# A frequency-domain mixer and a hash-routed expert layer on one core: mixed rows in token order, gathered by lists of token numbers

## The chip, the cores and the metric

The kernel runs on one core of one Trainium2 chip. The metric is the device time of one execution in microseconds, the median of three timed runs. The profile is of one further execution, whose span (first to last instruction) is somewhat shorter than the timed figure.

## The reference

Eight batches of 2496 tokens with 256 channels are filtered along the sequence: a real FFT, a product with a complex filter per frequency and channel, and the inverse FFT. The 19968 mixed rows then go through one of eight experts, chosen by the token's number alone.

```python
X = np.fft.rfft(x, axis=1)                     # x: (8, 2496, 256)
Y = X * (filt_r + 1j * filt_i)[None]
rows = np.fft.irfft(Y, n=2496, axis=1).reshape(19968, 256)

expert_idx = token_ids * 2654435761 % 8        # the low three bits of token_ids, in another order
for e in range(8):
    mask = expert_idx == e
    out[mask] = np.maximum(rows[mask] @ w1[e], 0.0) @ w2[e]      # 256 -> 1024 -> 256, float32
```

## The kernel before

**Mixing.** 2496 is 39 times 64, so each transform is done as matmuls with small tables, in four products per batch: `pa` (stage 1), `pb` and `pc` (stage 2, with the filter between them) and `pd` (stage 3). Between them the data goes through DRAM (`d1`, `d2`), because the next product needs another axis in the partitions: `load1` brings x, `load2` brings `d1`, `load4` brings `d2`. One batch has 44 matmuls of 256 columns in `pa`, 40 in `pb`, 40 in `pc` and 44 in `pd`.

**Routing.** From the token numbers the vector engine counts tokens per expert and gives each token a slot, so that the tokens of one expert lie in tiles of 128 rows. There are 163 tiles. Rows without a token (896 of them) are filled by seven scatters of a blank. The tiles are put in four groups (in the code: stages, by `STAGES = (2, 4, 6, 8)`): a tile of the first group holds tokens of the first two batches alone, one of the second group tokens of the first four, and so on, so that the expert layer can begin when two batches are mixed.

**Stage 3 and the scatter.** Each result row is written with a tag (its own token number, 16 words wide) straight to its slot in `xs`, a row of 272 words. GpSimd issues one indirect DMA for 117 rows:

```python
def stage3(self, u):
    n = min(XG, HN + 1 - XG * u)
    o = opool.tile([NR, XG, W], F32, ...)              # W = 256 + 16, two buffers
    nc.vector.tensor_scalar(o[:, 0:n, C:].bitcast(I32), tokno[...], float(self.b * S), None, op0=OP.add)
    copy = nc.scalar.copy if self.b < 2 else nc.vector.tensor_copy
    self.products(wi_t, ..., o, copy, u, "pd")
    for i in range(n):                                 # four per unit, 22 per batch
        scatter(o[0:r, i, :], sidx[0:r, self.b, j:j + 1], f"xs_{self.b}")
```

**The tiles.** A tile is loaded with one plain DMA, transposed (`xps`, `xt`), multiplied up (`ups`: 32 matmuls of 128 columns), put through the ReLU (`ht`), multiplied down (`dps`: 16 matmuls of 256 columns) and scattered to the output by the tags that came with it. Pieces of the mixing of the later batches lie between the two products:

```python
def load(i):
    q = tiles[i]
    xg[i] = gath.tile([P, W], F32, ...)                # eight buffers
    ld = nc.sync.dma_start(out=xg[i][:], in_=xs[q * TB:(q + 1) * TB, :])
    # waits for the batches of the tile's group, not for later ones

for i in range(NT):
    if i + 4 < NT:
        load(i + 4)
    up(i, ht)
    weights(i + 2, 0)                                  # loaded only where the expert changes
    if i + 1 < NT:
        turn(i + 1)
    while main and main[0][0] < i + 1:                 # pieces of mixing, by a table of times
        main.pop(0)[1]()
    down(i, ht)                                        # ends with the scatter to out, on GpSimd
    weights(i + 2, 1)
```

**Before the first tile** lies everything with a negative time in a table, in order: the mixing of batches 0 and 1, stage 1 of batch 2 and the first three units of its stage 2, the routing, and the load of the first two experts' weights.

```python
for v in range(NV):
    batches[0].load1(v)                                # x of batch 0 on the sync queue
...
todo = part1(0, spaced(-153, -143, NU)) + [(-152.5, count), (-152.4, route)]
todo += [(-154, lambda: load_tables(0)), (-129.5, places)]      # tables and filters on GpSimd and ACT queues
todo += part2(0, spaced(-128, -95, N_2), -142)
todo += part1(1, spaced(-123.5, -105, NU), [-141.5, -135, -134.5])   # last list: when x of batch 1 is loaded
todo += [(-118.2 + .1 * i, lambda i=i: (weights(i, 0), weights(i, 1))) for i in range(2)]
todo += part2(1, spaced(-94, -60, N_2), -103) + part3(0, spaced(-84, -51, NU), -94.5)
todo += part3(1, spaced(-54, -21, NU), -62) + part1(2, spaced(-52, -19, NU), [-85, -80, -41])
...
todo += part2(2, [-16, -12, -8] + spaced(.1, 5.5, N_2 - 3), -18) + part2(3, spaced(8.5, 15.5, N_2), 7)
```

Of the kernel before, what the change touches and what calls it, by code (L numbers as in the profile page):

```python
# [11 lines left out]
F32 = mybir.dt.float32  # L12
# [29 lines left out]

TB = 128
NT = (N + E * (TB - 1)) // TB
W = C + 16
NJ = N // P
# [50 lines left out]
def route_table():  # L97


    t = np.zeros((P, G + 2 + NQP + HN + 1), np.float32)  # L100
    p = np.arange(P)
    r = np.arange(NR)
    t[:NR, G + 2 + NQP:] = (N2 * (r % N1) + np.array(H0)[r // N1])[:, None] + np.arange(HN + 1)
    for g, b in enumerate(STAGES):
        t[:, g] = p < b * S // NJ
    order = sum(stage_tiles(), []) + [NT] * (2 * P - NT)
    t[:, G:G + 2] = np.array(order).reshape(2, P).T
    t[:, G + 2:G + 2 + NQP] = p[:, None] * NQP + np.arange(NQP)
    return t
# [3 lines left out]
def kernel(  # L113
# [16 lines left out]

    xs = nc.dram_tensor("xs", (NT * TB, W), F32)
    slot_dram = nc.dram_tensor("slots", (N,), I32)
# [22 lines left out]
    sidx = keep.tile([NR, B, HN + 1], I32)  # L155
    tokno = keep.tile([NR, HN + 1], F32)
# [7 lines left out]
    class Batch:  # L164


        def __init__(self, b):
            self.b = b
            self.d1 = self.d2 = None
            self.x, self.t2, self.t4, self.p = {}, {}, {}, {}  # L170
            self.g = None
# [112 lines left out]
        def stage3(self, u):  # L284

            n = min(XG, HN + 1 - XG * u)
            o = opool.tile([NR, XG, W], F32, name=f"o_{self.b}_{u}", tag="o")
            nc.vector.tensor_scalar(o[:, 0:n, C:].bitcast(I32),
                                    tokno[:, XG * u:XG * u + n].unsqueeze(2).to_broadcast([NR, n, W - C]),
                                    float(self.b * S), None, op0=OP.add)  # L290
# [4 lines left out]
            for i in range(n):  # L295
                j = XG * u + i
                r = NR if j < HN else N1
                scatter(o[0:r, i, :], sidx[0:r, self.b, j:j + 1], f"xs_{self.b}")

    def scatter(rows, index, group):  # L300
        st = nc.gpsimd.indirect_dma_start(  # L301
            out=xs[:], out_offset=bass.IndirectOffsetOnAxis(ap=index, axis=0),
            in_=rows, in_offset=None, bounds_check=NT * TB - 1, oob_is_err=False)
        for other in ["xs_pad", "xs_read"] + [f"xs_{b}" for b in range(B)]:
            tc.declare_no_dep(st.ins, group=other, reason="distinct rows")
        tc.add_to_no_dep_group(group, st.ins)

# [28 lines left out]
    tok = rpool.tile([P, NJ, 2], I32)  # L336
    nc.scalar.dma_start(tok[:], tok_h.bitcast(I32).rearrange("(p j two) -> p j two", p=P, two=2))
    rt = rpool.tile([P, G + 2 + NQP + HN + 1], F32)
    nc.scalar.dma_start(out=rt[:], in_=r_dram.ap())
    nc.vector.tensor_copy(tokno[:], rt[0:NR, G + 2 + NQP:])  # L340
# [3 lines left out]
    def load_tables(part):  # L344
        sl = S_PARTS[part]
        nc.gpsimd.dma_start(out=d_t[:, sl, :], in_=d_dram.ap()[:, sl, :])
        for k in range(2):
            load_filter(k, sl)

    def load_filter(k, sl):  # L350
        filt = (filt_r, filt_i)[k]
        for q in range(2):
            off, step = (0, C) if q == 0 else (N1 * C, -C)
            (nc.gpsimd if k or sl.start else nc.scalar).dma_start(
# [17 lines left out]
    make_identity(nc, ident[:])  # L372
    sign = rpool.tile([P, 1], F32)
# [17 lines left out]
    def count():  # L391

        eid_i = rpool.tile([P, NJ], I32)
        nc.vector.tensor_scalar(eid_i[:], tok[:, :, 0], E - 1, None, op0=OP.bitwise_and)
        eid = rpool.tile([P, NJ], F32)
        nc.vector.tensor_copy(eid[:], eid_i[:])
        mask = rpool.tile([P, E, NJ], F32)
        nc.vector.tensor_tensor(mask[:], eid[:].unsqueeze(1).to_broadcast([P, E, NJ]),
                                over(iota_e[:], NJ), op=OP.is_equal)
        maskf = mask[:].rearrange("p e j -> p (e j)")  # L400
        run = rpool.tile([P, E, NJ], F32)
        nc.vector.tensor_tensor_scan(run[:].rearrange("p e j -> p (e j)"),
                                     ones[:, 0:1].to_broadcast([P, E * NJ]), maskf, 0.0,
                                     op0=OP.mult, op1=OP.add)
        ends = rpool.tile([P, E + 1], F32)
        nc.vector.memset(ends[:, 0:1], 0.0)
        nc.vector.tensor_copy(ends[:, 1:], run[:, :, NJ - 1])
        cnt = rpool.tile([P, E], F32)
        nc.vector.tensor_sub(cnt[:], ends[:, 1:], ends[:, 0:E])
        cntg = rpool.tile([P, G, E], F32)  # L410
        nc.vector.tensor_tensor(cntg[:], cnt[:].unsqueeze(1).to_broadcast([P, G, E]),
                                rt[:, 0:G].unsqueeze(2).to_broadcast([P, G, E]), op=OP.mult)
        ps = fps.tile([P, 2, C], F32, name="cnt_ps", tag="f")
        nc.tensor.matmul(out=ps[:, 0, 0:G * E], lhsT=ones[:, 0:P], rhs=cntg[:].rearrange("p g e -> p (g e)"),
                         start=True, stop=True)
        nc.tensor.matmul(out=ps[:, 1, 0:E], lhsT=before[:], rhs=cnt[:], start=True, stop=True)

        rv.update(eid=eid, eid_i=eid_i, mask=mask, run=run, ends=ends, ps=ps)

    def route():  # L420
# [4 lines left out]
        nc.vector.tensor_copy(upto[:].rearrange("p g e -> p (g e)"), ps[:, 0, 0:G * E])  # L425
# [25 lines left out]
        base = rpool.tile([P, E], F32)  # L451
        nc.vector.tensor_sub(base[:], ps[:, 1, 0:E], ends[:, 0:E])
# [4 lines left out]
        acc = rpool.tile([P, E, NJ], F32)  # L457
        tmp = mask
        for e in range(E):
            nc.vector.scalar_tensor_tensor(run[:, e, :], run[:, e, :], base[:, e:e + 1], mask[:, e, :],  # L460
# [236 lines left out]
```

## Time and profile before

| what | value |
|---|---|
| timed, median of three (lowest, highest) | 1643.16 us (1642.09, 1643.37) |
| span of the profiled execution | 1629.8 us |
| TensorE matmul busy | 1518.8 us, 93% of the span |
| VectorE, ScalarE, GpSimd busy | 539.0, 217.1, 355.7 us |
| first matmul | at 15.7 us |
| first tile's first `ups` matmul | at 207.7 us |
| indirect DMAs by GpSimd | 176 to `xs`, 7 blanks, 163 to `out` |

"Busy" counts the time in which an engine executes; an engine that waits is not busy. A row of the profile's groups names a source line, the engine, the operation, what it writes and reads, how often it ran, its total and mean time, and then the idle time of the engine just before it with what ended that. The clock is TensorE's granted clock, 1.00 being full speed. A DMA share of 1.00 means that all 16 DMA engines are occupied.

### The profile page before, as it was taken

Reading aid. Unit: us, or ns where it says so; the run is one execution under the profiler, and the core shown is the slowest. Engines: PE = TensorE matmul, PEld = TensorE weight load, DVE = VectorE, ACT = ScalarE, POOL = GpSimd, SP = SyncE. Lnnn points to the kernel's source line nnn. Section 1 sums busy time; section 2 is a strip of 40 time slices with the busy share of each in tenths; the row PEclk is TensorE's granted clock in tenths of the full one; section 3 lists DMA queues with packets and bytes.
Section 4 is the critical chain, followed back from the end, with each engine's and each line's share of the span. In section 5 each row is a group of like instructions: output and inputs, shape, how many; then the busy total and the mean of one; then the engine's idle time right before and its main releaser. Section 6 shows DMA issues by size and latency. Waiting matters only on the chain.

```text
span 1629.8 us, 26685 instructions
## 1 busy us (share of the span) xinstructions
PE 1518.8 (93%) x9522; PEld 1381.7 (85%) x9522; DVE 539.0 (33%) x1022; ACT 217.1 (13%) x371; POOL 355.7 (22%) x375
## 2 busy tenths in 40 slices
PE   3676589999999999999999999999999999999997
PEld 2554378988888999899989998999999999999997
DVE  6572142452244444233434442222122121221221
ACT  2322212112111111111111111000000000000000
POOL 0235300331320132122121322233111111111111
PEclk9788699999999999999999999999999999999999
DMA  7998627747864883674537643544152413132220
GB/s 189 306 290 244 198 98 205 240 165 207 245 218 150 244 256 111 194 197 147 185 114 222 199 135 115 147 127 162 45 203 79 140 37 126 52 94 88 84 84 9
DMA packets 152541, 258.77 MB, mean 159 GB/s; under 512 B 16185, under 2 KB 118508, under 8 KB 150410
## 3 DMA queue, kind: packets, MB, share of 16 engines
q1 hardware_dynamic: 103345, 163.46, 33.1%
q0 software_dynamic: 21136, 50.96, 9.4%
q10 hardware_dynamic: 27928, 42.65, 8.3%
q8 instruction: 76, 1.25, 0.3%
q14 instruction: 56, 0.45, 0.1%
HBM read 431.87 MB, written 86.09 MB: 318 GB/s over the span
## 4 chain that ended last, share of the span: by engine, by line
PE 42%; issue 36%; POOL 7%; DMA 3%; DVE 2%; POOLq 1%; ACT 0%; SPq 0%; ACTq 0%; DVEq 0%
PE ups L630 15%; PE dps L642 15%; POOL out_dram L646 6%; PE pb L240 3%; PE pa L203 3%; PE pc L263 3%; PE pd L203 2%; POOL xs L301 2%; DMA xs<-o,sidx 1%; PE xps L619 1%; DVE z L250 1%; PE pa L198 0%; POOLq L646 0%; DMA d<-g 0%; DVE y L247 0%
## 5 line engine op out<-in xcount | busy, mean ns | idle before, releaser
L630 PEld LDWEIGHTS ups<-xt,w 128*128 128x128 f32 x5216 | 610.3, 193 | 9.2 <-DVE xt L621 1.0
L630 PE MATMUL ups<-xt,w 128*128 128x128 f32 x5216 | 611.1, 276 | 0.6 <-DVE xt L621 0.6
L642 PE MATMUL dps<-w,ht 128*128 128x256 f32 x2608 | 591.0, 380 | 0.0
L642 PEld LDWEIGHTS dps<-w,ht 128*128 128x128 f32 x2608 | 490.0, 191 | 63.7 <-issue 1.6
L646 POOL DMA_INDIRECT out_dram<-osb,xg x163 | 159.6, 979 | 944.6 <-DVE osb L645 919.4
L636 DVE TENSOR_SCALAR ht<-ups 128x512 f32<-128x512 f32 x163 | 112.8, 692 | 526.8 <-PE ups L630 519.7
L634 ACT ACTIVATE ht<-ups 128x512 f32<-128x512 f32 x163 | 97.3, 597 | 1008.0 <-PE ups L630 992.3
L301 POOL DMA_INDIRECT xs<-o,sidx x176 | 175.3, 996 | 245.7 <-DVE o L205 145.7
L645 DVE COPY osb<-dps 128x256 f32<-128x256 f32 x163 | 69.3, 425 | 404.5 <-PE dps L642 396.2
L240 PE MATMUL pb<-t,d_t 128*128 128x256 f32 x320 | 91.1, 413 | 23.8 <-DMA t<-d 23.3
L250 DVE TENSOR_TENSOR z<-pb,filt 64x512 f32<-64x512 f32 x160 | 110.1, 688 | 2.2
L263 PE MATMUL pc<-y,e_t 128*128 128x256 f32 x320 | 90.1, 407 | 19.7 <-DVE y L251 19.3
L240 PEld LDWEIGHTS pb<-t,d_t 128*128 128x128 f32 x320 | 63.5, 209 | 35.5 <-issue 25.9
L263 PEld LDWEIGHTS pc<-y,e_t 128*128 128x128 f32 x320 | 63.3, 203 | 35.8 <-issue 17.5
L203 PE MATMUL pd<-t,wi_t 120*117 120x256 f32 x320 | 81.2, 399 | 11.7 <-DMA t<-d 7.1
L203 PEld LDWEIGHTS pd<-t,wi_t 120*117 120x117 f32 x320 | 58.9, 191 | 25.5 <-issue 9.1
L247 DVE TENSOR_TENSOR y<-pb,filt 128x512 f32<-128x512 f32 x80 | 55.3, 691 | 68.3 <-PE pb L240 67.8
L266 ACT COPY g<-pc 128x512 f32<-128x512 f32 x80 | 46.8, 585 | 233.2 <-PE pc L263 229.8
L621 DVE COPY xt<-xps 128x256 f32<-128x256 f32 x163 | 67.6, 415 | 1.9 <-PE xps L619 1.9
L619 PE MATMUL xps<-ident,xg 128*128 128x128 f32 x326 | 62.6, 274 | 3.1 <-DMA xg<-xs 3.1
L203 PE MATMUL pa<-x,wf_t 117*120 117x256 f32 x264 | 63.3, 383 | 0.6 <-DVE z L250 0.6
L205 ACT COPY t<-pa 120x512 f32<-120x512 f32 x80 | 46.0, 588 | 90.6 <-PE pa L203 88.1
(102 smaller groups left out, 352.5 us busy)
## 6 DMA issues: line engine op xcount, KB each, us to landing
w<-in_moe_w_dram SPq DMA_DIRECT2D x322, 1024.0 KB
xg<-xs SPq DMA_DIRECT2D x163, 136.0 KB
t<-d SPq DMA_DIRECT2D x80, 256.0 KB
d<-g ACTq DMA_DIRECT2D x80, 256.0 KB
d<-t ACTq DMA_DIRECT2D x16, 960.0 KB
t<-d SPq DMA_DIRECT2D x16, 960.0 KB
x<-in_x_dram SPq DMA_DIRECT2D x39, 312.0 KB
x<-in_x_dram SPq DMA_DIRECT2D x21, 234.0 KB
```

The lines of the kernel that those rows point to most:

```text
L203: nc.tensor.matmul(out=ps[0:cols * H, k, :], lhsT=w[:], rhs=src[:, 2 * i + k, :], start=True, stop=True)
L240: nc.tensor.matmul(out=ps[:, i, :], lhsT=d_t[:, s, :], rhs=self.t2[s // SG][:, s % SG, :], start=True, stop=True)
L250: nc.vector.tensor_tensor(out=z[b], in0=ps[a], in1=f_t[1][a, sl, :], op=OP.mult)
L263: nc.tensor.matmul(out=ps[:, i, :], lhsT=e_t[:, 2 * u + i, :], rhs=pr[:, i, :], start=True, stop=True)
L301: st = nc.gpsimd.indirect_dma_start(out=xs[:], out_offset=bass.IndirectOffsetOnAxis(ap=index, axis=0), in_=rows, in_offset=None, bounds_ch ...
L619: nc.tensor.transpose(out=ps[:, dp, :], in_=xg[i][:, dp * P:(dp + 1) * P], identity=ident[:])
L630: nc.tensor.matmul(out=ps[:, k, :], lhsT=w1[:, dp, fp * P:(fp + 1) * P], rhs=xt[i][:, dp, :], start=(dp == 0), stop=(dp == DP - 1))
L634: nc.scalar.activation(out=dst, in_=ps[:], func=AF.Relu)
L636: nc.vector.tensor_scalar_max(dst, ps[:], 0.0)
L642: nc.tensor.matmul(out=ps[:], lhsT=ht[:, fp, :], rhs=w2[:, fp, :], start=(fp == 0), stop=(fp == FP - 1))
L645: nc.vector.tensor_copy(out=o[:], in_=ps[:])
L646: st = nc.gpsimd.indirect_dma_start(out=out[:], out_offset=bass.IndirectOffsetOnAxis(ap=xg[i][:, C:C + 1].bitcast(I32), axis=0), in_=o[:], ...
```

## The change

The mixed rows are stored in token order with plain DMAs from the scalar engine's queue, three for a unit of four rows. What is scattered instead is a list: one entry of 16 words for each slot, which holds the token's number. A tile loads its list (two tiles' lists in one plain DMA) and gathers its 128 rows with an indirect DMA; the same list then serves the scatter to the output. The lists depend on the token numbers alone, so they can be written before any row is mixed. For this the routing counts by pairs of batches (`G` = 4 groups of 39 columns instead of 156 columns in one), and the lists of one pair are 39 indirect DMAs of 128 entries. The schedule ahead of the first tile is laid out anew: the second part of the tables waits for x, x of batch 1 is asked for early, the weights later, and no stage 2 of batch 2 comes before the first tile.

```diff
-W = C + 16
-NJ = N // P
+LW = 16
+NJ = N // (4 * P)
...
-    xs = nc.dram_tensor("xs", (NT * TB, W), F32)
-    slot_dram = nc.dram_tensor("slots", (N,), I32)
+    mixed = nc.dram_tensor("mixed", (N + 1, C), F32)
+    lists = nc.dram_tensor("lists", (NT * TB, LW), I32)
... stage 3
-            o = opool.tile([NR, XG, W], F32, name=f"o_{self.b}_{u}", tag="o")
-            nc.vector.tensor_scalar(o[:, 0:n, C:].bitcast(I32), ...)
+            o = opool.tile([NR, XG, C], F32, name=f"o_{self.b}_{u}", tag="o")
-            for i in range(n):
-                scatter(o[0:r, i, :], sidx[0:r, self.b, j:j + 1], f"xs_{self.b}")
+            last, self.o = self.o, (o, u)
+            if last and self.b >= 2:
+                self.store3(*last)
+            if self.b < 2 or u == NU - 1:
+                self.store3(o, u)
+        def store3(self, o, u):
+            for h in range(H):
+                st = nc.scalar.dma_start(out=... mixed, rows of 4 KB ..., in_=o[N1 * h:N1 * h + N1, 0:n, :])
+    def listed(g, j0, j1):
+        if j0 == 0:
+            nc.gpsimd.iota(number[:], pattern=[[1, NJ], [0, LW]], base=P * NJ * g, channel_multiplier=NJ)
+        for j in range(j0, j1):
+            scatter(number[:, j, :], slots[:, g, j:j + 1], f"lists_{g}")
... tables
+        eng = nc.sync if part == 0 else nc.gpsimd
+        if part:
+            nc.gpsimd.tensor_copy(junk[:], batches[0].x[1][0:1, 0, 0:1])     # waits for x
... the table of times
-    todo = part1(0, spaced(-153, -143, NU)) + [(-152.5, count), (-152.4, route)]
-    todo += [(-154, lambda: load_tables(0)), (-129.5, places)]
+    todo = part1(0, spaced(-155, -143, NU)) + [(-152.5, count), (-152.4, route), (-152.3, places)]
+    todo += [(-154.9, lambda: load_tables(0)), (-154.8, lambda: load_tables(1))]
-    todo += part1(1, spaced(-123.5, -105, NU), [-141.5, -135, -134.5])
-    todo += [(-125, tile_experts), (-121, experts), (-108, blanks)]
+    todo += part1(1, spaced(-129, -105, NU), [-150, -149, -136])
+    todo += [(-140, tile_experts), (-130, experts), (-60, blanks)]
+    todo += [(-142, lambda: listed(0, 0, NJ))]
-    todo += [(-118.2 + .1 * i, lambda i=i: (weights(i, 0), weights(i, 1))) for i in range(2)]
-    todo += part2(1, spaced(-94, -60, N_2), -103) + part3(0, spaced(-84, -51, NU), -94.5)
-    todo += part3(1, spaced(-54, -21, NU), -62) + part1(2, spaced(-52, -19, NU), [-85, -80, -41])
+    todo += [(-82 + .1 * i, lambda i=i: (weights(i, 0), weights(i, 1))) for i in range(2)]
+    todo += part2(1, spaced(-100, -70, N_2), -103) + part3(0, spaced(-92, -73, NU), -97)
+    todo += part1(2, spaced(-70, -60, NU), [-104, -103.9, -78]) + part3(1, spaced(-59.5, -48, NU), -66)
-    todo += part2(2, [-16, -12, -8] + spaced(.1, 5.5, N_2 - 3), -18) + ...
+    todo += part2(2, spaced(.1, 7.4, N_2), -40) + ...
-    todo += part3(2, spaced(7, 14, NU), 5.6) + ...
+    todo += part3(2, spaced(8, 14, NU), 7.5) + ...
+    for g, (t0, t1) in enumerate([(1, 23), (30, 62), (70, 102)]):
+        todo += [(t, lambda g=g, j=j: listed(g + 1, j, j + 1)) for j, t in enumerate(spaced(t0, t1, NJ))]
... the tiles
-        xg[i] = gath.tile([P, W], F32, name=f"xg_{i}", tag="xg")
-        ld = nc.sync.dma_start(out=xg[i][:], in_=xs[q * TB:(q + 1) * TB, :])
+        if i % 2 == 0:
+            lst[i] = gath.tile([P, 2, LW], I32, name=f"lst_{i}", tag="lst")
+            ld = nc.sync.dma_start(out=lst[i][:, 0:n, :], in_=... lists of tiles i and i + 1 ...)
+        xg[i] = gath.tile([P, C], F32, name=f"xg_{i}", tag="xg")           # six buffers
+        ld = nc.gpsimd.indirect_dma_start(
+            out=xg[i][:], out_offset=None, in_=mixed[0:rows, :],
+            in_offset=bass.IndirectOffsetOnAxis(ap=lst[i // 2 * 2][:, i % 2, 0:1], axis=0), ...)
```

## The prediction

> **What bounds the kernel now.** I read the table of stretches first, then the groups of instructions, then the chain of waits and the timeline around the first tile.
>
> The table of stretches gives, for each stretch, its length, busy time and count of each engine, the granted clock, the DMA share and the rate. I set the borders at the places where the work changes:
>
> ```profile
> 0.00:40.00 40.00, 15.81 (x56) 12.20 (x56) 24.73 (x70) 10.84 (x16) 3.29 (x14) 0.94 0.71 187
> 40.00:125.00 85.00, 62.21 (x224) 47.37 (x224) 56.22 (x96) 23.80 (x38) 24.94 (x30) 0.83 0.95 300
> 125.00:150.00 25.00, 14.49 (x46) 9.86 (x46) 8.27 (x15) 5.41 (x11) 14.64 (x15) 0.75 0.81 244
> 150.00:182.00 32.00, 21.01 (x82) 15.78 (x81) 1.32 (x6) 11.17 (x22) 20.61 (x21) 0.87 0.71 208
> 182.00:207.70 25.70, 10.85 (x27) 6.49 (x26) 8.71 (x13) 1.99 (x5) 1.09 (x2) 0.57 0.65 204
> ...
> 222.00:700.00 478.00, 465.35 (x2888) 422.45 (x2887) 186.56 (x332) 74.69 (x130) 111.24 (x112) 1.00 0.64 198
> 700.00:1157.00 457.00, 452.38 (x2945) 418.32 (x2944) 153.94 (x290) 49.24 (x84) 116.71 (x118) 1.00 0.50 154
> 1157.00:1617.00 460.00, 460.00 (x3184) 434.44 (x3183) 91.64 (x190) 38.21 (x64) 62.22 (x64) 1.00 0.28 90
> ```
>
> There are two regimes. From 222 us on TensorE is busy nearly without a break (its first number against the length: 465 of 478, 452 of 457, 460 of 460), the DMA share is at most 0.64, and nothing but TensorE work counts. Before 207.7 us TensorE is busy for 124 us, at a lowered clock, and the DMA engines are full for the middle 85 us (0.95).
>
> The groups tell what a tile is made of, and how GpSimd stands:
>
> ```profile
> L630 PE MATMUL ups<-xt,w 128*128 128x128 f32 x5216 | 611.1, 276 | 0.6 <-DVE xt L621 0.6
> L642 PE MATMUL dps<-w,ht 128*128 128x256 f32 x2608 | 591.0, 380 | 0.0
> L646 POOL DMA_INDIRECT out_dram<-osb,xg x163 | 159.6, 979 | 944.6 <-DVE osb L645 919.4
> L301 POOL DMA_INDIRECT xs<-o,sidx x176 | 175.3, 996 | 245.7 <-DVE o L205 145.7
> L619 PE MATMUL xps<-ident,xg 128*128 128x128 f32 x326 | 62.6, 274 | 3.1 <-DMA xg<-xs 3.1
> ```
>
> TensorE waited 3.1 us in all for a tile's rows, so loads are hidden in the main part. In the timeline the first `ups` matmuls of successive tiles without mixing are 7.245 us apart, and eight mixing matmuls add 1.72 to 1.73 us, or 0.2155 us each. Over the main part this adds up: 163 tiles at 7.245 us are 1181 us; of the 6 x 168 = 1008 mixing matmuls of batches 2 to 7, 44 + 20 were done before, so 944 at 0.2155 us are 203 us; together 1384 us. The measured stretch from 207.7 to the end of the last `dps` near 1620.5 is 1413 us. So 29 us are other losses, of which 3.9 are in the first tile, at a cold clock, and most of the rest in tiles that hold two units of stage 2 one after the other. There is little to gain in the main part; **the change has to pay ahead of the first tile**.
>
> There the chain of waits names the scatters:
>
> ```profile
> 147.42 7.23 DMA xs<-o,sidx
> ...
> 162.35 7.05 DMA xs<-o,sidx
> ...
> 174.58 5.51 DMA xs<-o,sidx
> ...
> 185.16 4.27 DMA d<-t
> ...
> 190.54 3.18 DMA t<-d
> ...
> 201.63 4.66 DMA xg<-xs
> ```
>
> In this view each line is start, length, what. Stage 3 of batch 1 (147 to 182 us) writes into two buffers `o`, and a buffer is free only when its four scatters have been issued (one every 1.3 us: 0.99 busy and 0.30 until the next) and have landed. From 185 us on the chain is the write and reload of `d1` of batch 2 for three units of stage 2, then the tile's own load, which stands on the sync queue behind them.
>
> **What the Trainium skill says.** "DMA: Bandwidth & Descriptors", section "Issuing engines are not separate DMA queues", says that transfers issued by different engines all run on the same 16 DMA engines and interleave; moving the row stores from GpSimd to the scalar engine's queue thus saves issue time, not transfer time. The trace agrees for 40 to 125 us, where three queues together stand at a share of 0.95. The same page's "Specifications" puts transfers under 512 B below line rate, because the engine then reads, modifies and writes. A list entry is 64 B; no run here shows its cost yet. "TensorE: Matmul & The Clock Gate", section "What's actually happening", says that the clock halves after an idle window of about 3.4 us; the trace agrees, with 0.57 granted from 182 to 207.7 us, where waits of 9.5 and 3.1 us lie between TensorE's pieces.
>
> **The change part by part.**
>
> *First matmul.* It waits for x until 15.7 us while about 1.5 MB of tables and filters are asked for by other queues at the same time. At the 187 GB/s of that stretch, x of the first third (0.94 MB) plus a fair part of the rest is what takes so long. With the tables behind x I expect the first matmul near 10 us: -5.
>
> *Stage 2 of batch 0.* Before, its matmuls run from 41 us to 107 in the timeline, with the second half of the filters arriving at 63 to 68 us and x of batch 1 asked for at 38 to 51. Both now come earlier, and 4 MB of weights come later. I take its end at 92 us: -15, the -5 above included.
>
> *Stage 3 of batch 1.* Before, six units in 35 us. After, a unit has copies of 1.1 us, three store issues of about 0.5 us, and a landing of about 4 us (the write of `d1` took 4.27), and two buffers: (1.1 + 1.5 + 4) / 2 = 3.3 us a unit, 20 us in all: -15, of which I count 14.
>
> *From the last row to the first tile.* Before, 25.7 us (182 to 207.7). After, the last store lands (4 us), the gather is issued (1.3), lands (3.7, the median landing of the scatters to `xs`), and transpose and copy take 1.2 as now: about 11 us, -14.
>
> *Given back.* Three units of stage 2 of batch 2 (20 matmuls) move behind the first tile: +4.3 in the main part. Lists: 39 scatters at 1.3 us are 51 us on GpSimd; GpSimd is idle for most of 40 us to 110 us, so this lies beside other work, but they are 4992 small writes in the stretch where DMA is full. Weights (4.2 MB, 14 us at 300 GB/s) now fall into stage 2 of batch 1. I give back 16 us for both.
>
> Sum ahead of the first tile: -15 - 14 - 14 + 16 = -27, so it starts at 181 us. As a check by bytes: the stretches sum to 51.0 MB up to 207.7 us. The new order needs about 49.5 (blanks -1.0, tags -0.3, x of batch 3 less, lists +0.35). By 181 us that is a mean of 273 GB/s, below the 300 of the full stretch and above the 246 of before. At 300 GB/s it would be 165 us, at 246 it would be 201.
>
> *Main part.* GpSimd gets two indirect DMAs a tile instead of one, and while lists are written (39 in 22 tiles) 1.8 more: 3.8 x 1.3 = 4.9 us of at least 7.245. A gather is asked for four tiles ahead, some 29 us, and needs 2 + 1.3 + 4. The vector engine loses 48 tag writes (9.2 us), off the path. The scalar engine gains 18 issues a batch, and is at 13%. I take 0 for all this.
>
> Time: 1643.2 - 27 + 4.3 = 1620.5, rounded to **1621 us**.
>
> **Rivals.** (1) *DMA takes the place of the scatters.* If the transfers ahead of the first tile run at the old mean, because the lists' small writes cost as much as whole rows, the tile starts near 200 us and the time is 1640. For it: share 0.95 for 85 us. Against it: the share falls to 0.71 and 0.65 after 150 us, where the new order has no scatter to wait for. (2) *GpSimd becomes the bound.* Its queue is in order, and a gather stands behind list scatters and behind the scatter to the output of an earlier tile, which waits for that tile's end. If a gather came late by 1 us in each tile, it would cost 163 us. The lead of four tiles speaks against it; a loss at the three borders between groups, of up to 10 us each, is likelier (1650). (3) *The full rate is kept.* With no landing to wait for, the stretch runs at 300 GB/s, the tile starts at 165 us and the time is 1605.
>
> **Range and chances.** The start lies between 164 and 202 us by these, which is 1603 to 1642. Faster by over 2% needs less than 1610.3, a start before 170.5: 0.22. Slower by over 2% (above 1676) needs rival 2 in full: 0.04. Within 2%: 0.74.
>
> **What would show it.** The first `ups` matmul near 181 us; a first `pa` near 10 us; no wait of a copy for a scatter in stage 3, but short ones for stores to `mixed`; a DMA share of 0.85 or more up to 150 us; tiles still 7.245 us apart, with under 5 us in all of TensorE waiting for `xg`. The prediction is wrong if the share is near 1 and the start is still about 200, if tiles after 222 us are longer than 7.245, or if TensorE waits at tiles 30, 70 or 108.

## The result: slower by 4.3%, and the profile after

The changed kernel takes **1712.53 us** (median of four runs, 1707.16 to 1716.71) against 1642.62 us before (four runs, 1639.85 to 1643.37): 1.0427 times as long, 95% interval 1.0394 to 1.0460. The prediction was 1621 us, with a range up to 1642. It was wrong in sign: the change made the kernel slower.

The table of stretches of the kernel after, in the columns known from before (start and end, length, busy time of TensorE, its weight loads, VectorE, ScalarE and GpSimd, granted clock, DMA share, GB/s):

```profile
0.00:40.00 40.00, 14.58 (x56) 10.89 (x56) 29.66 (x73) 9.58 (x16) 7.72 (x20) 0.81 0.85 238
...
60.00:80.00 20.00, 0.21 (x1) 0.00 (x0) 1.40 (x3) 0.58 (x1) 15.38 (x16) 0.56 0.04 9
...
92.00:136.00 44.00, 29.06 (x106) 21.48 (x105) 23.84 (x33) 15.21 (x23) 1.73 (x3) 0.77 0.78 261
136.00:191.00 55.00, 39.80 (x125) 28.83 (x126) 29.34 (x50) 11.62 (x22) 0.00 (x0) 0.78 0.59 163
191.00:247.70 56.70, 27.86 (x91) 19.25 (x89) 0.42 (x1) 13.13 (x25) 10.32 (x11) 0.71 0.73 211
...
700.00:1200.00 500.00, 492.22 (x3165) 452.07 (x3164) 168.38 (x298) 57.92 (x100) 173.66 (x171) 1.00 0.51 153
```

The stretch from 60 to 80 us has no counterpart before: TensorE works for 0.21 us of 20, the DMA engines are at a share of 0.04, and GpSimd alone is busy, issuing list scatters (15.38 us). The stretch from 136 to 191 is stage 2 of batch 1. In the kernel before, the same work lies here:

```profile
98.00:135.00 37.00, 28.48 (x114) 22.18 (x112) 28.25 (x44) 10.25 (x18) 15.14 (x15) 0.93 0.89 278
```

VectorE does about the same in both (29.34 and 28.25 us), but in 55 us instead of 37, and with the DMA engines at 0.59 instead of 0.89: the stage now waits for something other than transfers at full rate. TensorE, with a granted clock of 0.78 instead of 0.93, is busy for 39.80 us instead of 28.48.

The groups of instructions of the kernel after:

```profile
L658 PE MATMUL ups<-xt,w 128*128 128x128 f32 x5216 | 611.6, 276 | 0.7 <-DVE xt L649 0.7
L670 PE MATMUL dps<-w,ht 128*128 128x256 f32 x2608 | 596.6, 382 | 5.8 <-DMA w<-in_moe_w_dram 4.7 <-issue 1.1
L636 POOL DMA_INDIRECT xg<-mixed,lst x163 | 173.3, 1063 | 387.7 <-DMA lst<-lists 140.1 <-issue 77.1 <-PE pa L198 38.9
L304 POOL DMA_INDIRECT lists<-number,slots x156 | 155.6, 997 | 72.2 <-issue 47.0 <-DVE slots L495 24.3 <-POOL number L314 0.8
L647 PE MATMUL xps<-ident,xg 128*128 128x128 f32 x326 | 62.5, 274 | 7.1 <-DMA xg<-mixed,lst 7.1
```

The tiles cost what they cost before. The gathers wait 140.1 us for their lists on GpSimd, but TensorE waits only 7.1 us in all for gathered rows (3.1 before). New is the wait of `dps` for weights (4.7 us; it was 0.0 for anything).

The chain of waits ahead of the first tile (start, length, what) names where the time lies:

```profile
13.99 20.28 DMA d<-t
...
67.96 21.85 another core or an unknown queue
...
146.19 8.13 DMA d<-g
...
177.50 2.83 DMA mixed<-o
180.36 14.71 issue
...
199.09 13.49 DMA t<-d
...
219.51 6.21 DMA t<-d
225.74 5.11 DMA mixed<-o
...
232.82 4.78 DMA mixed<-o
...
243.43 2.78 DMA xg<-mixed,lst
```

The write of `d1` of batch 0 takes 20.28 us. The 21.85 us at 68 are in the stretch where everything stands still. At 146 a store to `mixed` waits for an earlier store to `d2`. From 180 on, SyncE's queue stands at the last third of x of batch 2, with the read of `d2` of batch 1 behind it; the loads of x are issued from 195.07 on, the read at 199.09, and it takes 13.49 us to land. Not all of the 14.71 us are lost to the order: the last stores to `d2` are issued at 191.47, and by the semaphore records they had landed near 194.5, so the read was held some 4.6 us by x. The last step, from gather to tile, is short.

By the first and last matmul of each product, and with the start of the first tile's `ups`, the same in a table (the last column is a further run of the changed kernel, e9, told below):

| step | before | after | e9 |
|---|---|---|---|
| first `pa` | 15.7 | 8.0 | 10 |
| end of stage 2 of batch 0 | 98 | 130 | 96 |
| end of stage 2 of batch 1 | 135 | 191 | 168 |
| start of stage 3 of batch 1 | 148 | 212.7 | 190.9 |
| last matmul of stage 3 of batch 1 starts | 181.1 | 238.6 | 216.5 |
| first `ups` | 207.7 | 247.7 | 225.7 |

The first tile is 40 us later than before. The timed medians differ by 70 us, which leaves 30 for what follows. But the old kernel's profiled execution took 1631.37 us, 11 less than its median, so profile against profile what follows is 45 us longer; where those 11 us lie is not recorded.

### The profile page after: what moved, and what is told of

Its sections match the earlier page's. It is cut to its first block, busy times and chain, and to the rows that moved or that the text cites. A ratio compares the mean times of both kernels' runs of the same rounds, so it can differ in the third digit from the quotient of the medians.

```text
span 1715.1 us, 27107 instructions
## 1 busy us (share of the span) xinstructions
PE 1538.2 (90%) x9522; PEld 1388.9 (81%) x9522; DVE 534.9 (31%) x970; ACT 216.8 (13%) x371; POOL 508.9 (30%) x515
## 4 chain that ended last, share of the span: by engine, by line
PE 82%; DMA 7%; issue 4%; DVE 3%; another core or an unknown queue 2%; ACT 1%; SPq 1%; ACTq 0%; POOL 0%; POOLq 0%; DVEq 0%
PE ups L658 33%; PE dps L670 32%; PE pd L198 4%; PE pc L258 4%; PE pa L198 4%; PE pb L235 3%; DMA d<-t 2%; DMA t<-d 2%; PE xps L647 2%; DVE z L245 1%; DMA mixed<-o 1%; DMA d<-g 1%; DVE y L242 1%; PE pd L193 0%
## 5 line engine op out<-in xcount | busy, mean ns | idle before, releaser
L674 POOL DMA_INDIRECT out_dram<-osb,lst x163 | 161.8, 993 | 628.3 <-DVE osb L673 603.7
L636 POOL DMA_INDIRECT xg<-mixed,lst x163 | 173.3, 1063 | 387.7 <-DMA lst<-lists 140.1
L304 POOL DMA_INDIRECT lists<-number,slots x156 | 155.6, 997 | 72.2 <-issue 47.0
L198 PE MATMUL pd<-t,wi_t 120*117 120x256 f32 x320 | 87.9, 422 | 17.2 <-DMA t<-d 7.6
```

The costliest lines, as they stand in the source:

```text
L198: nc.tensor.matmul(out=ps[0:cols * H, k, :], lhsT=w[:], rhs=src[:, 2 * i + k, :], start=True, stop=True)
L304: st = nc.gpsimd.indirect_dma_start(out=lists[:], out_offset=bass.IndirectOffsetOnAxis(ap=index, axis=0), in_=rows, in_offset=None, bounds ...
L636: ld = nc.gpsimd.indirect_dma_start(out=xg[i][:], out_offset=None, in_=mixed[0:rows, :], in_offset=bass.IndirectOffsetOnAxis(ap=lst[i // 2 ...
L674: st = nc.gpsimd.indirect_dma_start(out=out[:], out_offset=bass.IndirectOffsetOnAxis(ap=lst[i // 2 * 2][:, i % 2, 0:1], axis=0), in_=o[:], ...
```

## The experiments

Each group of runs below shared one chip and one run of the kernel before on it; the groups ran on different chips, so kernels are compared within a group only. All but g1 are single runs, and differences under some 5 us are not read.

### Group 1: are the list scatters, and their small rows, what costs? (before: 1633.36)

**e1 and e2**: the kernel before with 39 more scatters (of 64-byte rows in e1, of 1088-byte rows in e2) to a spare tensor, between `places` and the weights on GpSimd's queue.

```diff
-(-129.5, places)
+(-129.5, places), (-129.4, burst)      # 39 indirect DMAs of 128 rows, 16 or 272 words each
```

> The kernel before, with 39 indirect scatters of 128 rows of 64 bytes added right after the slots are known, into a DRAM tensor that nothing reads (nothing is left out). Theory L (a run of small list writes holds up the other engines): a gap of 20 to 35 us in which DVE, ACT and TensorE stand still while GpSimd scatters, signals of TensorE that reach their waiters about 10 us late, first tile 20 to 35 us later than 207.7 us, time about 1665 to 1680. Theory T (order of tables and x alone is to blame for the later start): no gap, time within 10 us of before, since GpSimd's 50 us lie beside other work. In both the weights of the first experts come about 50 us later than before, which should not reach the first tile.

> The same 39 scatters, with rows of 1088 bytes instead of 64 (the size of the rows that the kernel before scatters to xs). If the smallness of the rows is what holds the engines up (theory L): no gap with late signals, but 5.4 MB more traffic in the full stretch, some 18 us at 300 GB/s, time about 1655 to 1662. If it is the run of 39 scatters without a pause, whatever their size: the same gap as with 64 bytes or a longer one, time 1670 or more.

Measured: 1658.54 and 1659.89 us, first `ups` at 235.2 and 236.6. A run of 39 scatters costs 25 us, and the size of the rows costs nothing that can be seen. "DMA: Bandwidth & Descriptors", section "Specifications", of the Trainium skill puts transfers under 512 B below line rate; at one scatter in 1.28 us these runs show no difference between 64 B and 1088 B. What costs is what stands behind: in e1 the weights are issued at 114 us instead of 57, land beside stage 2 and 3, and the next row scatters, which signal the same semaphores, wait for them (14.4 us in three waits). Those row scatters free the buffers of stage 3, and TensorE waits 27.3 us at one `pb` for the copies into them. The changed kernel has no row scatters, so this cost is not its own.

**e3**: the changed kernel without list and blank scatters; five plain DMAs at the start fill the lists in slot order, so the tiles gather the rows of other tokens, and rows go to wrong experts. The amount of work in the tiles is unchanged.

```diff
-            scatter(number[:, j, :], slots[:, g, j:j + 1], f"lists_{g}")
+    nc.gpsimd.dma_start(out=lists[...], in_=number[:, 0:n, :])      # five of these, no scatter
```

> The kernel after, without its 156 list scatters and 7 blank scatters; the lists are instead filled at the very start by five plain DMAs with the slot's own number, so that tiles gather rows in slot order (the rows go to the wrong experts; the gathers, the list loads and the scatters to the output are all there). Theory L: the gap from 60 to 90 us is gone, first tile about 215 to 225 us instead of 247.7, and the losses in tiles 8 to 23 shrink from about 45 us to about 20; time 1655 to 1670. Theory T: first tile still later than 235 us; time above 1690. If the gathers were to blame for the main part, its loss stays at 40 us or more over the pure sum.

Measured: 1667.95 us, first `ups` at 222.75. The change still costs 35 us, but the stand-in is not free: the routing now waits behind the five plain DMAs on GpSimd, and TensorE stands still for 23.21 us at the routing's counts:

```profile
38.84 0.60 PE L434 MATMUL cnt_ps<-cnt,ones 128*128 128x32 f32 x2 [23.21 <-DVE cnt L432]
```

The first `pb` comes at 61.6 us (50 in the kernel after). So this run doesn't price the lists.

**e4**: the changed kernel with the second part of the tables and x of batch 1 asked for later.

```diff
-(-154.8, lambda: load_tables(1))        x of batch 1 at [-150, -149, -136]
+(-129.45, lambda: load_tables(1))       x of batch 1 at [-131, -127, -126]
```

> The kernel after, with x of batch 1 and the second part of the tables asked for about when the kernel before does it, not ahead of stage 2 of batch 0. Theory T: the first stage 1 is no longer held up by slow writes of d1 (20.3 us to landing), stage 2 starts near 41 us instead of 50.2, and the time falls by 10 to 25 us. Theory L: stage 2 starts earlier, but then meets the same run of list writes from 38 us on; the gap stays, and the time changes by less than 8 us.

Measured: 1700.69 us. Stage 1 of batch 0 ends at 28 us and the first `pb` comes at 36.1 (50 after), so the 20 us write of `d1` was indeed held up by those loads. But the tables now stood behind the 39 list scatters on GpSimd's queue, and VectorE waited 43.9 us for filter rows. The edit was confounded; g1 tries the order of these loads alone, in the old kernel. No signal came late in e4, though all 39 list scatters ran; but TensorE had little to finish in those 43.9 us.

### Group 2: the same kernel again, lists later, stores elsewhere (before: 1644.59)

**e5**: the changed kernel unchanged. 

> The kernel after, unchanged, on the chip of this group of runs. In its profile TensorE's signals reached their waiters about 10 us late three times between 57 and 90 us, while GpSimd wrote lists; the 64-byte writes added to the kernel before did not show this. If that gap belongs to the kernel, it is there again and the time is 1705 to 1717. If it was a disturbance of single executions, the gap is gone, the first tile comes near 215 to 225 us and the time is 1660 to 1675.

Measured: 1716.96 us, first `ups` at 244.3, with the same standstill from 57 to 90 us. It is therefore no chance event of one execution. ScalarE's timeline of the kernel after shows it (start, length, instruction, in brackets the idle time before it; "remote" means that the records show no releaser close by):

```profile
57.57 0.58 ACT L200 COPY t<-pa 120x512 f32<-120x512 f32 x1 [16.20 <-PE pb L235]
67.38 0.58 ACT L200 COPY t<-pa 120x512 f32<-120x512 f32 x1 [9.22 <-remote]
89.83 0.58 ACT L261 COPY g<-pc 128x512 f32<-128x512 f32 x1 [21.87 <-remote]
```

The two `pa` groups and the `pc` group that these copies wait for, and a `pb` group for which VectorE waits until 78.58, end between 55 and 60 us by TensorE's records. They are taken up at 57.6, 67.4, 78.6 and 89.8 us: in order, and ten to eleven us apart. "Perfetto Trace Analysis", section "Tensor Engine Instruction (MATMUL, LD_WEIGHTS)", of the Trainium skill says that the end of a matmul in a profile is computed from its size and that the signal follows only when PSUM has acknowledged the writes. So the records can't tell a late signal from a matmul that truly took so long. I call them late signals.

**e6**: the first lists behind the first weights on GpSimd.

```diff
-(-142, lambda: listed(0, 0, NJ))
+(-81, lambda: listed(0, 0, NJ))
```

> The kernel after, with the 39 list scatters of the first group moved on GpSimd's queue behind the load of the first weights, so that they run from about 95 to 145 us and not from 37 to 87. If the run of list scatters beside stage 2 of batch 0 makes the gap: no gap at 57 to 90 us, first tile 15 to 30 us earlier, time 1680 to 1695, unless the gap moves with the lists to 110 to 145 us. If the lists have nothing to do with it: first tile within 5 us of after.

Measured: 1711.98 us, first `ups` at 235.3. The lists are now scattered from 65 to 117 us, and the late signals moved with them, to 93, 97, 102, 114 and 122 us:

```profile
70.00:80.00 10.00, 8.69 (x39) 7.17 (x38) 6.47 (x10) 3.61 (x7) 5.93 (x7) 0.95 0.87 305
...
90.00:100.00 10.00, 2.11 (x5) 1.13 (x6) 0.41 (x1) 0.96 (x2) 7.56 (x9) 0.57 0.16 59
```

From 70 to 80 us TensorE runs well; from 90 to 100, still beside scatters, it does a quarter of that. The lateness comes with a run of list scatters, but only some 10 to 25 us into it.

**e7**: the 144 stores to `mixed` issued by GpSimd instead of ScalarE. (The edit also drops the line that frees a store from waiting for gathers of other batches' rows.)

```diff
-                st = nc.scalar.dma_start(out=... mixed ...)
+                st = nc.gpsimd.dma_start(out=... mixed ...)
```

> The kernel after, with the 144 stores to mixed issued by GpSimd instead of the scalar engine. In the trace the DMAs of the sync and the scalar engine share eight completion semaphores in turn, so that a store waits until the eighth DMA before it has landed, and the scalar engine with it. If these waits are what makes stage 2 of batch 1 and tiles 8 to 23 longer (theory S): the scalar engine's waits for transfers fall, stage 2 of batch 1 takes about 40 us instead of 50, the losses in the tiles fall by 10 us or more, time 15 to 30 us less than after. If not: within 8 us of after.

Measured: 1693.99 us, 23 less than e5; first `ups` at 234.1 instead of 244.3. Stage 2 of batch 1 takes 42 us (135.8 to 177.4) instead of 54, and in the groups the wait of `dps` for weights is gone:

```profile
L669 PE MATMUL dps<-w,ht 128*128 128x256 f32 x2608 | 597.7, 382 | 3.4 <-DVE ht L663 2.7 <-issue 0.7
```

In e5 the same row had 5.0 us for weights, all in tile 22. The reason for that one is in the trace's semaphore records: in this program, transfers issued by SyncE and ScalarE signal eight semaphores in rotation, and the issue of one waits until the transfer eight before it has landed. Three more stores per unit on ScalarE bring that forward, for SyncE's loads of weights and `d2` too. GpSimd's transfers have eight of their own. But in e7 TensorE waits 6.74 us in tile 23 for a copy of stage 3, so tiles 22 and 23 together are only 2.4 us shorter than in e5.

The shorter stage 2 can be put down to the stores: the weights, which now stand behind them on GpSimd and are issued at 168 to 173 us, had in e5 all moved by 107 us, well ahead of this stage. In TensorE's groups for stage 2 of batch 1 (130 to 191 us of e5, 130 to 177.5 of e7), the row of `pc` shows what went:

```profile
L258 PE MATMUL pc<-y,e_t 128*128 128x256 f32 x40 | 13.5, 470 | 11.6 <-DVE z L245 6.8 <-DVE y L246 3.4 <-DVE held L517 1.3
L258 PE MATMUL pc<-y,e_t 128*128 128x256 f32 x41 | 13.3, 452 | 3.8 <-DVE y L246 2.5 <-DVE held L516 1.3
```

The 6.8 us are three waits of 2.28 us for VectorE. Every run of the changed kernel with the stores on ScalarE has them; e7 has none. Why a wait for VectorE goes with ScalarE's stores is not shown.

**e8**: the kernel before with only the loads of the change (tables on SyncE behind x of batch 0; x of batch 1 early). 

> The kernel before, with only the loads of the change: x first, then the first part of the tables from the sync queue, the second part after x has landed, x of batch 1 asked for early. Theory T (this order delays stage 2): the first matmul comes near 8 us, but d1 of batch 0 is written slowly, stage 2 starts near 50 us instead of 41, first tile 5 to 15 us later, time 1638 to 1650 against a before of 1633. If the order is what I predicted it to be, a gain: first tile 5 to 15 us earlier, time 1618 to 1628.

Measured: 1638.35 us, 6 less than the kernel before; the first `pa` at 9 us, but the first `pb` at 52 (41 before), and stage 2 of batch 0 ends at 97.

### Group 3: a chip without late signals (before: 1640.68)

**e9**: the changed kernel unchanged. 

> The kernel after, unchanged, as the control of this group. In the two profiles of after, TensorE finished its matmuls only every 10 us while GpSimd wrote the first lists; in four runs of another group on another chip no such thing was seen. If it comes with the kernel, it is here too, and the time is 1705 to 1717. If it comes with the chip, it is here only where the kernel before takes about 1644 us and not about 1633, and otherwise after takes 1670 to 1690.

Measured: **1676.99 us**, 36 over the kernel before instead of 72, without late signals. The stretch of the standstill, and stage 2 of batch 1:

```profile
60.00:80.00 20.00, 15.26 (x75) 12.52 (x75) 15.03 (x21) 10.46 (x15) 15.46 (x15) 1.00 0.48 138
...
107.00:168.00 61.00, 38.73 (x124) 27.93 (x125) 29.10 (x49) 11.68 (x21) 0.00 (x0) 0.75 0.63 186
```

GpSimd issues the same run of lists (15.46 us busy), and TensorE works beside it at full clock. So the run of lists alone does not stop it. But stage 2 of batch 1 is longer still than in the kernel after (61 us from its first `pb`, against 55). From e9's chain:

```profile
106.31 18.40 DMA t<-d
...
176.74 14.02 DMA t<-d
```

The first is the read of `d2` of batch 0, which the trace has landing beside 4.2 MB of weights (each load 20.1 us from issue to landing) that stood behind the lists until 93 us; 2.15 MB of them moved after 107 us, in this stage. In the kernel after, whose stage 2 of batch 1 started at 136, all the weights had moved by 106 us. The second is the read of `d2` of batch 1, as in the chain of the kernel after.

**e10**: without list and blank scatters, as e3, with the plain DMAs behind the tables. 

> As the earlier kernel without list scatters, but with the five plain fills behind the tables on GpSimd's queue, not ahead of them (rows again in slot order; wrong experts, same work otherwise). Against the control of the same chip: if list scatters hold TensorE up, the first tile is 20 to 30 us earlier and the losses in the tiles fall by 15 to 20 us, so 35 to 50 us less time. If they don't, less than 10 us.

Measured: 1673.93 us, 3 less than e9, which is within the noise. The stand-in again moves two things. VectorE, which takes part in filling the lists, holds TensorE up for 13.89 us at 69 us, and stage 2 of batch 0 ends at 114 instead of 96. The weights are issued at 74 to 81 us and have all moved by 96, and stage 2 of batch 1 then ends 59 us after that of batch 0 instead of 72. So the 3 us are a sum of opposite shifts and don't price the scatters. What the lists cost is better seen in e9 itself: beside the whole run of them, stage 2 of batch 0 ended at 96, against 98 in the kernel before.

**e11**: e1 on this chip. 

> The kernel before with 39 scatters of 64-byte rows, repeated on this group's chip. On the other chip it cost 25 us, all of it by the place of the first weights on GpSimd's queue, without any late signal of TensorE. If the chip decides: where the control shows late signals, this one shows them too between 50 and 110 us, and it costs 40 us or more. If the kernel decides: again about 25 us and no late signals.

Measured: 1657.63 us, first `ups` at 234.4 as in e1, and no late signal. It costs 17 us here (25 in e1).

**e12**: the changed kernel with stage 3 of batch 2 two tiles later.

```diff
-part3(2, spaced(8, 14, NU), 7.5)
+part3(2, spaced(9.9, 15.5, NU), 7.5)
```

> The kernel after, with stage 3 of batch 2 moved from tiles 8 to 14 to tiles 9.9 to 15.5 (its loads stay). In after TensorE waits 5.9 us in tile 8 for d2 of batch 2, which stage 2 has just written, because three units of stage 2 were moved behind the first tile. If that is the cause of the 9 us lost in tile 8: 6 to 9 us less than the control. If something else then waits in its place: within 3 us.

Measured: 1665.43 us, 11.6 less than e9, with the first `ups` at the same place (225.5). TensorE's timeline in tile 8 of e9 had this line, and e12 has no such wait there:

```profile
328.36 3.76 PE L198 MATMUL pd<-t,wi_t 120*117 120x256 f32 x8 [6.04 <-DMA t<-d]
```

Stage 2 of batch 2 starts only behind the first tile, so its `d2` is complete later than before, while the first piece of stage 3 stood in tile 8.

### Group 4: why stage 2 of batch 1 is longer (before: 1640.94)

**f1**: the changed kernel unchanged. 

> The unchanged kernel after the change, as the control of this group. Theory: about 36 us over the kernel before where TensorE's signals come on time (pc of batch 1 ends 56 us after its first piece, first ups near 226), about 72 us over it where they come late (first ups near 245).

Measured: 1725.86 us, first `ups` at 249.2; late signals again, at 58, 69, 80 and 91 us.

**f2**: the weights behind the first 20 list scatters instead of all 39.

```diff
-(-142, lambda: listed(0, 0, NJ))
+(-142, lambda: listed(0, 0, 20)), (-80, lambda: listed(0, 20, NJ))
```

> Edit: the first 20 list scatters stay where they are, the other 19 move behind the four weight loads on GpSimd, so that the weights are asked for some 25 us earlier (near 67 us, as in the kernel before). Theory W (the weights land in stage 2 of batch 1 and hold up its reads of d1 and the reads of d2 for stage 3): pb of batch 1 starts about 10 us earlier (near 97) and the whole stage is 8 us shorter, first ups about 12 to 15 us earlier than the control's. Rival S (the order of the pieces paces the stage): pb starts earlier but pc of batch 1 and the first ups move by under 4 us.

Measured: 1712.25 us, 13.6 less than f1; the first `pb` of batch 1 at 127.5 instead of 137.0, the first `ups` at 237.4 instead of 249.2. But that is not theory W. Stage 2 of batch 0 already ends at 120.6 instead of 130.8, and stage 2 of batch 1 takes 53.9 us from its first `pb` instead of 55.0, where theory W expected 8 less. In f1 the weights had all moved by 107 us, 30 us before that stage began, so on this chip they could not hold it up. The late signals now come in two bouts, one in each of the two runs of scatters, and between them (70 to 90 us) TensorE works for 16 us of 20; the gain lies there.

**f3**: the stages after stage 2 of batch 0 at their places of before.

```diff
-part2(1, spaced(-100, -70, N_2), -103) + part3(0, spaced(-92, -73, NU), -97)
-part1(2, spaced(-70, -60, NU), [-104, -103.9, -78]) + part3(1, spaced(-59.5, -48, NU), -66)
+part2(1, spaced(-94, -60, N_2), -103) + part3(0, spaced(-84, -51, NU), -94.5)
+part3(1, spaced(-54, -21, NU), -62) + part1(2, spaced(-52, -19, NU), [-85, -80, -41])
```

> Edit: stage 2 of batch 1, stage 3 of batches 0 and 1 and stage 1 of batch 2 (with its loads of x) go back to the places in the list of pieces that they had before the change; everything else as after. Theory S: with the change's order ScalarE alternates copies of stage 2 of batch 1 with those of stage 3 of batch 0, each of which waits about 10 us for the stores of two pieces earlier, so stage 2 runs at 6 us a piece instead of 3.4. With the old order stage 2 of batch 1 takes 40 to 45 us instead of 61; the first ups move by between -10 and +5 us, since the other stages stand further apart again. Rival W: stage 2 of batch 1 keeps 55 us or more.

Measured: 1724.36 us, first `ups` at 249.4, as f1. Stage 2 of batch 1 did get shorter (131 to 180, 49 us instead of 55), so the order has a part in it, but all of it was given back later.

**f4**: both edits. 

> Both edits of this group together. If both causes hold, stage 2 of batch 1 takes about 37 us as before the change and starts near 97; first ups at 205 to 215, the time about 15 to 20 us below the control's. If only one holds, it is within 4 us of that one's run.

Measured: 1709.15 us, first `ups` at 234.8. Stage 2 of batch 1 takes 43 us (122.7 to 166), 12 less than in f1. The gain of the order is lost again behind stage 3: its last matmul starts at 209.4, the tile comes 25.4 us later (9.2 in f1). SyncE's queue shows why (start, length, transfer):

```profile
217.80 3.69 SPq L227 DMA_DIRECT2D t<-d  x6
221.53 2.42 SPq L181 DMA_DIRECT2D x<-in_x_dram  x3
224.39 1.79 SPq L627 DMA_DIRECT2D lst<-lists  x3
```

With the old order, stage 1 of batch 2 ends late, SyncE waits for its `d1` at 217.8, and the first tile's list stands behind that. The new order exists to avoid this. ScalarE's timeline in e9 shows the pace of stage 2:

```profile
145.10 0.59 ACT L261 COPY g<-pc 128x512 f32<-128x512 f32 x1 [3.66 <-PE pc L258]
145.72 1.11 ACTq L265 DMA_DIRECT2D d<-g  x2
147.00 1.07 ACT L200 COPY o<-pd 117x512 f32<-117x512 f32 x2 [1.31 <-PE pd L198]
148.10 1.42 ACTq L296 DMA_DIRECT2D mixed<-o  x3
151.07 0.59 ACT L261 COPY g<-pc 128x512 f32<-128x512 f32 x1 [3.00 <-PE pc L258]
```

The copies of `g` (stage 2 of batch 1) are 6 us apart here, against 3.4 in the kernel before. The alternation with the copies of `o` (stage 3 of batch 0) is not enough to explain it: the kernel before alternates them too, and e7, with the new order kept, has the copies of `g` 3.2 to 4.2 us apart. Nor is it a wait for the buffer of `o`, as expected for f3: the copy at 147.00 reuses the buffer whose stores were issued from 136.5 on, and these had landed by 143.5 us by the semaphore records. In this stretch each `pc` starts late by the 2.28 us for VectorE that e7 doesn't have, and the copy of `g` waits for `pc`.

### Group 5: one part alone, and the run of scatters once more (before: 1636.76)

**g1**: the kernel before, with the first eight tables and filter rows on SyncE behind x of batch 0, and the other loads at their old places or close to them.

```diff
-        nc.gpsimd.dma_start(out=d_t[:, sl, :], in_=d_dram.ap()[:, sl, :])
+        eng = nc.sync if part == 0 else nc.gpsimd
+        if part:
+            nc.gpsimd.tensor_copy(junk[:], batches[0].x[1][0:1, 0, 0:1])
+        eng.dma_start(out=d_t[:, sl, :], in_=d_dram.ap()[:, sl, :])
```

> The kernel before, with one part of the change alone: the first eight tables and filter rows are asked for by SyncE right behind x of batch 0; x of batch 1 and the other tables keep their old places. It is meant to beat both kernels. Theory: first pa near 9 us instead of 15.7, and, since nothing else is asked for while stage 1 of batch 0 writes d1, the first pb near 36 instead of 41 (it was 52 where x of batch 1 and the other tables were asked for early too); the first ups 3 to 6 us earlier, the time 3 to 6 us lower. Rival: stage 2 of batch 0 is held by the transfers anyway, ends at 98 as before, and the time stays within 1 us.

Measured: **1627.07 us** (six runs), 0.9944 times the kernel before, interval 0.9922 to 0.9966. It beats both kernels. First `pa` at 9 us, first `pb` at 36 (41 before), first `ups` at 203.9 (207.7).

**g2**: e1 on a fifth chip. 

> The kernel before with a run of 39 scatters of 64-byte rows between places and the weights, on a further chip. Theory R (a run of scatters on GpSimd is by itself what makes TensorE's signals come ten us apart): on a chip of that kind stage 2 of batch 0 stands still for some 30 us, first ups near 265 and the time near 1690. Rival C (it needs more of the changed kernel, or a chip of that kind): first ups near 235 and the time near 1658, as on two chips already; without a run of the changed kernel on this chip the two readings of that outcome can't be told apart.

Measured: 1660.69 us, first `ups` at 237.0, no late signals; as e1 and e11. The changed kernel did not run on this chip, so this doesn't tell its two readings apart.

## Why the prediction was wrong, step by step

*What held.* The first matmul came at 8.0 us (predicted 10). With signals on time, stage 2 of batch 0 ended at 96 (predicted 92). The last row to the first tile took 9 us by the table (predicted 11, before 27). Tiles without mixing stayed 7.245 us apart, no tile waited at the borders between groups, and GpSimd did not become the bound, so rival 2 fell, and rival 3's full rate was nowhere near. TensorE's wait for `xg` was 7.1 us instead of under 5. Where signals were on time, the list scatters did not lengthen the stage beside them (e9); a run without lists that held nothing else up was not made.

*"Stage 2 of batch 0, -15".* The step failed at its start: I took 107 us as the old end, but the matmuls up to 107 include the first of batch 1. Batch 0's last `pc` is at 98, so down to the 92 that I expected only 6 us were to be had, and e9 got 2. In the kernel of the comparison, with late signals, it is +32.

*"Given back, 16" for lists and weights.* This term was mis-sized, and it missed the interaction. Stage 2 of batch 1, the stage it was meant for, ended 72 us after stage 2 of batch 0 in e9 and 61 after, against 37 before: +35 and +24. Two causes come out of the runs.

The first is the stores on ScalarE. I counted them as issue time on an engine at 13%. With the same stores on GpSimd the stage takes 42 us instead of 54 on the same chip (e7 against e5). More than half of these 12 us, 6.8, are waits of `pc` for VectorE and not waits for landings in ScalarE's queue. The order of the pieces has a smaller part, 6 us with everything else as after (f3 against f1); with the weights earlier as well it was 11 (f4 against f2), and hardly any of it reached the first tile.

The second is the place of the weights, and it applies in e9 alone. I had counted their bytes, but not that GpSimd's queue is in order and the lists stand before them. With signals on time half of them land beside the reads of `d1` and `d2`, for which TensorE waits 19.9 us in that stage; where they had moved before the stage began, it ended 59 us after that of batch 0 (e10, the same chip) or 61 (the kernel after), and not 72. I estimate them at 11 to 13 us from this difference.

*"Stage 3 of batch 1, -14".* From its first matmul to its last it takes 25.9 us instead of 33.1 (-7); a store lands in 4.8 to 5.1 us in the chain, not 4. But the new order puts stage 1 of batch 2 ahead of it, and SyncE's last load of x ahead of the read of `d2` (some 4.6 us). The gap between stage 2 and stage 3 is 21.7 us instead of 13: +9, a wait that no step of the prediction had. It was not tried alone.

*"Last row to the first tile, -14".* It came out at -17.5 (9.1 us instead of 26.6).

Together, for the kernel of the comparison: +32 + 24 + 8.7 - 7.2 - 17.5 = +40, against the predicted -27.

*"Main part, 0", beside +4.3.* In e9 everything after the start of the first tile is 18 us longer by the times of its group, and 27.6 us longer profile against profile. 4.3 were planned, 8.8 are tile 8 (e12 took 11.6 off the time), and 6.5 are tile 22, where `dps` waits for weights; in e7, where the stores no longer share their semaphores, that wait is gone, though another came in tile 23. I had taken the loads in the main part as hidden because they were hidden before, and did not follow what moving three pieces of stage 2 behind the first tile does to the piece of stage 3 that needs their result.

*What stays open.* In the comparison (whose chip is not on record) and on the chips of groups 2 and 4 the change costs 70 to 85 us, on that of group 3 36. The difference goes with late signals of TensorE: they appear beside runs of list scatters, moved with them (e6), split with them (f2), and were absent in e9 with the same run. Why some chips show them, whether a run of scatters does it by itself there, and whether it is the signal or the matmul that is late, these runs don't settle: the extra run of scatters in the kernel before (e1, e11, g2) never met a chip on which they had been seen.

## What to carry to other kernels

Where transfers, copies and loads of several stages share in-order queues, price a moved operation by what then stands behind it, in each queue and each semaphore rotation, and not by its issue time and bytes; here the lists and the gathers held up little where signals came on time, while moving the stores to ScalarE cost one stage 12 us (e7), and weights that came late beside its reads another 11 to 13 (an estimate, from e9 against e10 and the kernel after). Before taking a saving off a stage's end, check by its count of instructions that the end is that stage's. When a run is meant to show what a part costs, look where the stand-in for it is slow, and whether the stage that it should help is the one that got shorter: e3, e10 and f2 mislead without that. And take a change apart into its pieces before you judge it: one of its loads, alone in the old kernel, was worth 0.6%.

## What the runs showed of the hardware

In a run of 39 indirect scatters of 128 rows, GpSimd issues one every 1.28 us (median), with rows of 64 B as with rows of 1088 B (e1 and e2).

In this program, the issue of a transfer on ScalarE can wait for one of SyncE's, and the other way round, through the eight completion semaphores that both use in turn: a store to `mixed` waits 6.21 us for a load of `d1` (219.51 in the chain above), and SyncE's load of x waits 25.1 us until the store to `mixed` of 177.50 has landed.

In the comparison and in groups 2 and 4 (e5, f1), TensorE's groups were taken up by ScalarE and VectorE ten to eleven us apart while GpSimd issued list scatters, though the other engines and the DMA engines were nearly idle (DMA share 0.04); on the chip of group 3 they were not.
